# Scaling and saving the first two experts' weights on other engines and at other times, and routing the first batch right behind its convolution

## The chip, the cores and the metric

The kernel runs on one core of a Trainium2 chip. Each core has a matrix engine (TensorE, "PE"), a vector engine (VectorE, "DVE"), a scalar engine (ScalarE, "ACT"), a general engine (GpSimd, "POOL") and an engine that here only issues transfers (SyncE, "SP"). Every engine works through its own list of instructions in order, and waits at an instruction until what it needs is there. POOL also issues the transfers that gather and scatter rows. The metric is the device time of one execution in microseconds; lower is better.

## The reference: a causal convolution, then a mixture of experts

There are 8 sequences (batches) of 3584 tokens with 192 channels. Each of 8 heads convolves its 24 channels with 7 softmaxed taps. The result, 28672 rows, is then routed: a token with a positive skip score goes to the expert with its largest gate logit, and the expert's output, weighted by its gate probability, is added to the row.

```python
w = exp(weight - max); w = w / (sum(w) + 1e-9)          # 8 heads x 7 taps
out = einsum('hk,bskhg->bshg', w, x_unf)                # causal windows of 7 tokens
do_compute = x @ w_skip > 0
e_idx = argmax(xc @ w_gate); gate_w = softmax(...)[e_idx]
h = maximum(xc[mask] @ w1[e], 0)                        # 192 -> 1024
y[mask] = gate_w * (h @ w2[e])                          # 1024 -> 192
out[do_compute] = xc + y
```

## The kernel before, in words

**Two phases.** Phase one goes through the 8 batches (`phase1_step(b)`, b from 0 to 7). For each of the 8 heads of a batch, `conv_head` makes four fp32 matmuls into `pc` (line 301) and ACT copies them back over the input tile (line 304), so that the tile `xy` then holds the convolved rows. Phase two, "the tail", takes 64 blocks of up to 256 routed rows of one expert: POOL gathers their rows from DRAM (line 713), DVE and ACT split them into two fp16 parts (`prep`), SP transposes these by DMA (line 748), PE multiplies by W1 in `up` (line 792), ACT and DVE split the hidden values into `hh` and `hl` (lines 796 and 798), PE multiplies by W2 in `down` (lines 826 to 828), and POOL scatters the sums (line 810).

**Routing of a batch** is a chain written as generators that hand control back at each yield. `router` transposes the convolved rows on PE (line 356), copies them on ACT (line 357), multiplies by the gate weights (lines 363 and 366) and transposes the logits back (line 374). POOL makes an intermediate copy `yc` (line 337). `slots` works out on DVE which expert a token has (`lm` at line 412 to the one-hot `oh` at line 432), counts them with three matmuls (`pr`, lines 437 to 439), and gives each token its slot. Its line 445 also starts the store of the batch to DRAM (`store_y`, line 318). `invert` then turns slots into lists of rows: DVE builds one-hot tiles `oa`, `oj` and `ob` (lines 521 and 530) four times per batch, and PE sums them into `inv` (line 508). After batch 4 (`REL`), `tail_rows` reads `inv` and makes the row lists `rowsa` for the first 8 blocks, which belong to experts 0 and 1 (`NTAIL` is 8); they take the tokens of the batches up to 4. The next blocks of the two take rows from all batches.

**Weights.** The weights of an expert arrive as fp32 (`raw`, line 208) and are used as two fp16 parts. `split_weights(e, wt)` takes the maxima of seven pieces of 512 columns on DVE (line 216), a maximum over the partitions on POOL (`partition_all_reduce`, line 224), then makes a power of two scale `ar`, and for each of the seven pieces a scaled fp16 "high part" (for experts 0 and 1 on POOL, line 238; for the others on ACT, line 241) and the rest as the "low part" on DVE (`low_part`, line 254). There is one `raw` buffer. `save_weights` copies the finished parts of experts 0 and 1 to DRAM (`wscr`, line 262); the last blocks of the tail read any expert's weights from there.

**The order** is written out by tables of digits, one string per batch and one digit per head: `RR` says how often the routes are advanced behind that head, `IR` how often the inversion, `BGS` how many steps of the background list `bg` are run, which holds the generators of the weights. Before, a batch's route begins in the step of the following batch, one hop per head, so that PE's list alternates between the convolution of batch b, the transposes of batch b-1 and the inversion of batch b-2 or b-1. The order of each engine's instructions follows from the order in which these generators emit. `E1` is the batch in which the weights of expert 1 begin. In the tail, `background()` runs one step per slot.

**Buffers that tie the phases.** There are four row buffers for the batches, so batch b+4 is loaded when batch b is stored. The gather buffers `y` lie where the rows of batches 0 and 4 were; POOL clears them first (line 691). The buffers `hh` and `hl` lie where batches 1 and 5 were, so that the first `hh` of the tail waits until the last piece of batch 5 has landed in DRAM. A transfer that SP issues also waits until the transfer eight before it has landed.

Of the kernel before, what the change touches and what calls it, by code (L numbers as in the profile page):

```python
# [41 lines left out]
NA = 2  # L42
# [16 lines left out]
FIRST = ("0", "", "1", "", "2", "3", "", "")  # L59
WARM = (6, 58)  # L60

IR = ("00000000",) * 2 + ("11111112",) * 4 + ("11122222", "11111111")
RR = ("00000000",) + ("11111111",) * 7
BGS = ("40000000", "00000000", "11111111", "11122222", "11140000", "11111111", "11222222", "11111111")
PICK = "102"
E1 = 4
PIECES = (2,) * 5 + (8,) * 3

PSEQ = (0, 0, 3, 4, 4, 4, 4, 4)
# [20 lines left out]
def conv_router_moe(ctx: ExitStack, tc: tile.TileContext, x, band, taps, router_weights, weights, out):  # L90
    nc = tc.nc
# [57 lines left out]
    wra, wrb = wr[:, 0:2], wr[:, 2]  # L149
    nc.sync.dma_start(out=wr.rearrange("p j e -> p (j e)"), in_=router_weights)  # L150
    load_x(1)
    load_x(2)
    nc.vector.tensor_reduce(out=wkm, in_=wk, axis=AX.X, op=ALU.max)

    def over(t, n):
# [47 lines left out]
    def split_weights(e, wt):  # L203
# [30 lines left out]
        for k, (c0, c1, oh, ol, n) in enumerate(parts):  # L234
            for v in range(n):
                o = 512 * v
                if e < NA:
                    nc.gpsimd.tensor_scalar(out=wt[:, oh + o:oh + o + 512], in0=raw[:, c0 + o:c0 + o + 512],  # L238
                                            scalar1=ar[:, k:k + 1], scalar2=None, op0=ALU.mult)
                else:  # L240
                    nc.scalar.activation(wt[:, oh + o:oh + o + 512], raw[:, c0 + o:c0 + o + 512], AF.Copy,
                                         scale=ar[:, k:k + 1])
                if held:
                    low_part(*held)
                held = wt, raw, ar, e, k, c0 + o, oh + o, ol + o
                yield
                if e >= NA and (k, v) < (1, 1):
                    yield
# [336 lines left out]
    wts = {}  # L585
    bg = []
# [38 lines left out]

    def phase1_step(b):

        if b > 0:
            routes.append(whole_route(b - 1))
        if b in (0, E1):  # L630
            e = int(b == E1)
            wts[e] = new_wt(e)
            bg.append(split_weights(e, wts[e]))
        for h in range(H):
            if b > 0:
                conv_head(b, h)
            elif h == 0:
                first_batch()
            for i in range(max(int(RR[b][h]), int(IR[b][h]))):
                more = i < int(IR[b][h])  # L640
                if i < int(RR[b][h]):
# [14 lines left out]
            store_piece()  # L656
            if h == 6 and 2 <= b < B - 2:
                load_x(b + 2)
        if not b:
            load_x(3)  # L660

    def step7(h):

# [385 lines left out]
    ahead = []  # L1049
    while preps or begun[0] < PREP0:  # L1050
        prep_piece()
    bg.extend(save_weights(e, wts[e]) for e in range(NA))
    weave(up(blocks[0], weights_of(0)))
    for n in range(NBLK):
        k = blocks[n]
        if n == NTAIL:
            while not past:
                next(tables[0])
# [130 lines left out]
```

## Time and profile before

| | |
|---|---|
| median of 3 runs | 687.71 us (686.76 to 687.85) |
| profiled execution | 686.38 us, its span 684.7 us |
| mean granted TensorE clock | 0.967 |
| busy in the span: PE, DVE, ACT, POOL | 634.8, 490.5, 333.5, 290.1 us |
| phase one, to the first W1 matmul of the tail | 0 to 183.81 us |
| transition, PE all but idle | 187 to 193.71 us |
| tail | 193.71 to 684.7 us |
| moved by DMA | 136.87 MB, mean 200 GB/s |

In the rows of a timeline the first number is the start in microseconds from the span's start, the second the duration of the group, then come the engine, the line, the operation, the tile written and the tiles read, and xN the count; in brackets stands how long the engine had been idle before, and what ended that. In a table of stretches, each engine has its busy time and in brackets its instructions, PEclk is the granted clock as a share of full speed, DMA the mean busy share of the DMA engines. "issue" as a releaser means that the engine waited for nothing that the profile shows. A displayed duration holds some start-up that overlaps with the instruction before, so the distance between the starts of neighbours is a little shorter than the duration.

### The profile page before, as it was taken

The page shows a single profiled execution, that of the slowest core. Times are in us where ns is not written, and L with a number is a line of the kernel's source. Part 1 is how long each engine was busy: PE and PEld are TensorE (multiplying, and loading weights), DVE is VectorE, ACT ScalarE, POOL GpSimd, SP SyncE. Part 2 cuts the span into 40 slices and gives each one's busy share as a digit, 9 for nine tenths or more (in the row PEclk, how much of TensorE's full clock was granted, in tenths as well). Part 3 has the DMA queues.
Part 4 walks back from the last instruction along what each step waited for, and adds up shares of the span by engine and source line. Part 5 has one row for each costly group of instructions (what it writes and reads, how often), then busy time and mean ns, then how long its engine had stood idle before and what let it go on. Part 6 is the DMA issues. An engine that isn't in the chain of part 4 may idle for free.

```text
span 684.7 us, 18082 instructions
## 1 busy us (share of the span) xinstructions
PE 634.8 (93%) x6921; PEld 528.1 (77%) x6921; DVE 490.5 (72%) x1365; ACT 333.5 (49%) x666; POOL 290.1 (42%) x306
## 2 busy tenths in 40 slices
PE   7799599948769999999999999999999999999995
PEld 4456355524358999989999899999999899999995
DVE  2069397847758989787798788789788876666652
ACT  4587447734454333464463554554553634444321
POOL 2011441137204446365454554654555455554322
PEclk9999869998889999999999999999999999999998
DMA  8968659832586626276457365366464445999960
GB/s 354 424 269 351 256 195 412 316 129 73 143 325 214 205 65 193 63 202 188 79 171 194 82 183 179 109 166 162 126 207 118 119 140 174 297 313 292 288 206 15
DMA packets 93392, 136.87 MB, mean 200 GB/s; under 512 B 58300, under 2 KB 72574, under 8 KB 90864
## 3 DMA queue, kind: packets, MB, share of 16 engines
q1 hardware_dynamic: 82256, 112.92, 50.9%
q0 software_dynamic: 11040, 22.71, 11.8%
q8 instruction: 56, 0.92, 0.6%
q14 instruction: 40, 0.33, 0.2%
HBM read 73.24 MB, written 51.88 MB: 183 GB/s over the span
## 4 chain that ended last, share of the span: by engine, by line
PE 65%; DVE 5%; DMA 2%; POOL 1%; issue 1%; ACT 1%; SPq 1%; POOLq 0%; DVEq 0%; ACTq 0%
PE ph L792 29%; PE po L828 10%; PE po L826 10%; PE po L827 10%; PE ph L783 4%; DMA y<-out_dram,rowsa 1%; DVE hl L798 1%; PE tp L356 1%; POOL wt L238 1%; DVE oa L521 1%; DMA out_dram<-xy 0%; DVE yam L732 0%; ACT hh L796 0%; DVE yt L745 0%; POOL y L691 0%
## 5 line engine op out<-in xcount | busy, mean ns | idle before, releaser
L796 ACT ACTIVATE hh<-ph 128x512 f16<-128x512 f32 x230 | 130.8, 589 | 240.7 <-PE ph L792 227.7
L798 DVE SCALAR_TENSOR_TENSOR hl<-ph,hh 128x512 f16<-128x512 f32 x230 | 155.7, 685 | 57.1 <-ACT hh L796 55.4
L826 PE MATMUL po<-wt,hh 128*128 128x192 f16 x768 | 188.9, 246 | 0.0
L828 PE MATMUL po<-wt,hl 128*128 128x192 f16 x768 | 188.9, 246 | 0.0
L827 PE MATMUL po<-wt,hh 128*128 128x192 f16 x768 | 188.9, 246 | 0.0
L792 PE MATMUL ph<-m,wt 128*128 128x256 f16 (+1 forms) x1680 | 186.6, 269 | 1.0 <-DVE hl L798 0.6
L792 PEld LDWEIGHTS <-wt 128*128 128x128 f16 x1680 | 154.1, 98 | 26.3 <-issue 10.1
L810 POOL DMA_INDIRECT out_dram<-o,rows x82 | 87.3, 1065 | 126.4 <-DVE o L808 103.2
L713 POOL DMA_INDIRECT y<-out_dram,rows x82 | 85.2, 1039 | 25.5 <-issue 11.9
L827 PEld LDWEIGHTS <-hh 128*128 128x128 f16 x920 | 90.0, 98 | 0.6
L826 PEld LDWEIGHTS <-hh 128*128 128x128 f16 x920 | 90.0, 98 | 0.6
L828 PEld LDWEIGHTS <-hl 128*128 128x128 f16 x920 | 90.0, 98 | 0.0
L808 DVE SCALAR_TENSOR_TENSOR o<-po,yf,y 128x192 f32<-128x192 f32 x115 | 47.1, 415 | 48.7 <-PE po L828 46.3
L304 ACT COPY xy<-pc 128x768 f32<-128x768 f32 (+1 forms) x72 | 51.7, 728 | 44.1 <-PE pc L301 33.7
L301 PE MATMUL pc<-xy,toep 64*64 64x384 f32 (+1 forms) x576 | 61.0, 505 | 7.3 <-DMA xy<-in_x_dram 5.8
L745 DVE SCALAR_TENSOR_TENSOR yt<-y,ysc,yt 128x64 f16<-128x64 f32 x230 | 57.9, 311 | 2.9 <-ACT yt L740 2.9
L740 ACT ACTIVATE yt<-y,ysc 128x192 f16<-128x192 f32 x115 | 46.3, 447 | 22.6 <-DVE ysc L735 14.0
L254 DVE SCALAR_TENSOR_TENSOR wt<-raw,ar,wt 128x512 f16<-128x512 f32 x56 | 44.6, 806 | 13.6 <-POOL wt L238 13.6
L356 PEld LDWEIGHTS tp<-ident,xy 128*128 128x128 f32 x256 | 30.3, 151 | 25.2 <-issue 10.8
L337 POOL COPY yc<-xy 128x1024 f32<-128x1024 f32 x12 | 13.3, 1107 | 82.5 <-ACT xy L304 43.8
L356 PE MATMUL tp<-ident,xy 128*128 128x128 f32 x256 | 38.4, 297 | 6.6 <-ACT ya L357 6.6
L216 DVE TENSOR_REDUCE am<-raw 128x1 f32<-128x512 f32 x56 | 37.8, 676 | 2.0 <-DMA raw<-in_weights_dram 1.6
(183 smaller groups left out, 827.9 us busy)
## 6 DMA issues: line engine op xcount, KB each, us to landing
xy<-in_x_dram SPq DMA_DIRECT2D x7, 3200.0 KB
wd<-wscr SPq DMA_DIRECT2D x44, 449.0 KB
wscr<-wt SPq DMA_DIRECT2D x84, 128.0 KB
out_dram<-xy SPq DMA_DIRECT2D x21, 400.0 KB
raw<-in_weights_dram SPq DMA_DIRECT2D x16, 512.0 KB
out_dram<-xy SPq DMA_DIRECT2D x5, 1600.0 KB
out_dram<-xy SPq DMA_DIRECT2D x5, 1500.0 KB
raw<-in_weights_dram SPq DMA_DIRECT2D x16, 384.0 KB
```

The lines of the kernel that those rows point to most:

```text
L301: nc.tensor.matmul(pc[K1 * c:K1 * c + K1, r, 0:n * G], toep[K1 * r:K1 * r + K1, h, :], xy[K1 * r:K1 * r + K1, at:at + 2 * n - 1:2, h * G:( ...
L304: nc.scalar.copy(xy[:, 2 * i0:2 * i0 + 2 * n, h * G:(h + 1) * G].rearrange("p (i r) g -> p r i g", r=2), pc[:, :, 0:n * G].rearrange("p r ...
L356: nc.tensor.transpose(tp[:, u, :], src, ident)
L713: rows_apart(nc.gpsimd.indirect_dma_start(out=k.y[:, u, :], out_offset=None, in_=out[0:k.rows, :], in_offset=bass.IndirectOffsetOnAxis(ap= ...
L745: nc.vector.scalar_tensor_tensor(out=yt[:, u, o:o + b_ - a], in0=k.y[:, u, a:b_], scalar=sc[:, u:u + 1], in1=yt[:, u, a:b_], op0=ALU.mult, ...
L792: nc.tensor.matmul(ph[:, f - f0, :], wt[:, o + f * P:o + (f + 1) * P], k.m[:, m, 0:w], start=(n == 0 and not paired(k)), stop=(n == len(se ...
L796: nc.scalar.activation(hh, ph, AF.Relu)
L798: nc.vector.scalar_tensor_tensor(out=k.hl[:, f0:f0 + fs, 0:w], in0=ph, scalar=0.0, in1=hh, op0=ALU.max, op1=ALU.subtract)
L810: rows_apart(nc.gpsimd.indirect_dma_start(out=out[0:k.rows, :], out_offset=bass.IndirectOffsetOnAxis(ap=k.si[:, u:u + 1], axis=0), in_=o[: ...
L826: nc.tensor.matmul(pos[u], hh, w2(OW2, f), start=(f == 0), stop=False)
L827: nc.tensor.matmul(pos[u], hh, w2(OW2L, f), start=False, stop=False)
L828: nc.tensor.matmul(pos[u], hl, w2(OW2, f), start=False, stop=(f == NF - 1))
```

## The change

Four things are done at once.

- The loads of batches 2 and 3 are issued behind the load of expert 0's weights; before, batch 2 was ahead of these weights.
- The whole router of batch 0 is emitted in step 0, behind its convolution and ahead of the convolution of batch 1; its slots and its inversion begin in step 1. From batch 1 on, a route begins one step later, as before.
- The high parts of experts 0 and 1 are scaled on DVE instead of POOL. Their steps lie elsewhere: expert 0's maxima in steps 1 and 2 (before: step 2) and its scaling in step 3 (before: the end of step 3 and step 4), expert 1 begins in step 3 (before 4) and is scaled in step 6, one piece per head (before: in the last heads of step 6).
- The two experts' parts are saved to DRAM from the sixth block of the tail on (`n == NTAIL - 3`) instead of at its head.

```diff
-IR = ("00000000",) * 2 + ("11111112",) * 4 + ("11122222", "11111111")
-RR = ("00000000",) + ("11111111",) * 7
-BGS = ("40000000", "00000000", "11111111", "11122222", "11140000", "11111111", "11222222", "11111111")
+IR = ("00000000",) + ("11111112",) * 5 + ("11122222", "11111111")
+RR = ("11111111",) * 8
+BGS = ("00000000", "00111111", "11111111", "22222400", "11111111", "11111111", "11111111", "11111111")
 PICK = "102"
-E1 = 4
+E1 = 3
...
     load_x(1)
-    load_x(2)
...
                 if e < NA:
-                    nc.gpsimd.tensor_scalar(out=wt[:, oh + o:oh + o + 512], in0=raw[:, c0 + o:c0 + o + 512],
+                    nc.vector.tensor_scalar(out=wt[:, oh + o:oh + o + 512], in0=raw[:, c0 + o:c0 + o + 512],
                                             scalar1=ar[:, k:k + 1], scalar2=None, op0=ALU.mult)
...
     def phase1_step(b):
 
-        if b > 0:
+        if b > 1:
             routes.append(whole_route(b - 1))
         if b in (0, E1):
             e = int(b == E1)
             wts[e] = new_wt(e)
             bg.append(split_weights(e, wts[e]))
+        if b == 0:
+            background(4)
+            load_x(2)
+            load_x(3)
+            first_batch()
+            routes.append(whole_route(0))
         for h in range(H):
             if b > 0:
                 conv_head(b, h)
-            elif h == 0:
-                first_batch()
...
-        if not b:
-            load_x(3)
...
-    bg.extend(save_weights(e, wts[e]) for e in range(NA))
     weave(up(blocks[0], weights_of(0)))
     for n in range(NBLK):
         k = blocks[n]
+        if n == NTAIL - 3:
+            bg.extend(save_weights(e, wts[e]) for e in range(NA))
```

The change moves instructions on every engine. Three places follow, as the lists of the two kernels have them; line numbers of the changed kernel are one lower than before around here.

**PE, where the convolution of batch 0 ends** (`xy_102` is batch 0, `xy_180` batch 1). Before:

```order
L301 MATMUL pc_7_8_322<-xy_102,toep 64x192 x4
L301 MATMUL pc_0_0_335<-xy_180,toep 64x384 x4
L356 MATMUL tp_0_0_343<-ident,xy_102 128x128 x4
L356 MATMUL tp_0_1_349<-ident,xy_102 128x128 x4
L301 MATMUL pc_1_0_355<-xy_180,toep 64x384 x4
```

Of the change, the end of batch 0's router, after which the convolution of batch 1 begins:

```order
L355 MATMUL tp_1_5_430<-ident,yc_1_376 128x128 x4
L362 MATMUL pl_1_436<-ya_1_378,wr 32x256 x8
L365 MATMUL pl_1_436<-yb_1_423,wr 32x256 x4
L373 MATMUL pb_1_451<-ident,lt_1_449 128x128 x2
L300 MATMUL pc_0_0_456<-xy_180,toep 64x384 x4
L300 MATMUL pc_1_0_476<-xy_180,toep 64x384 x4
L436 LDWEIGHTS ones_105
L436 MATMUL pr_482<-oh_474,ones_105 128x31x8
L437 MATMUL pr_482<-hist,ones_214 128x8
```

The twelve groups of transposes and the products of batch 0 now stand in front of the first matmul that reads batch 1, and the convolution of batch 1 is interrupted by batch 0's counts (`pr`) and, further on, its inversion.

**DVE, where the low parts of expert 0's weights are made** (`raw_328` and `raw_230` are its fp32 weights, `raw_982` expert 1's; `oa`, `oj` and `ob` are the one-hot tiles of an inversion, the last of which PE waits for). Before, where step 3 passes into step 4, with the scaling itself on POOL:

```order
L530 TENSOR_TENSOR ob_8_990<-oj_8_989,vals_918 128x576
L254 SCALAR_TENSOR_TENSOR wt_231<-raw_328,ar_768,wt_231 128x512 x2
L521 TENSOR_TENSOR oa_16_1044<-ramp,rf_914 128x1024
L521 TENSOR_TENSOR oj_16_1045<-iota_j,qf_916 128x576
L530 TENSOR_TENSOR ob_16_1046<-oj_16_1045,vals_918 128x576
```

Of the change, in step 3, ahead of the first and second `ob` of batch 1:

```order
L520 TENSOR_TENSOR oa_0_936<-ramp,rf_929 128x1024
L520 TENSOR_TENSOR oj_0_937<-iota_j,qf_931 128x576
L237 TENSOR_SCALAR wt_229<-raw_230,ar_651 128x512
L253 SCALAR_TENSOR_TENSOR wt_229<-raw_230,ar_651,wt_229 128x512
L237 TENSOR_SCALAR wt_229<-raw_230,ar_651 128x512
L253 SCALAR_TENSOR_TENSOR wt_229<-raw_230,ar_651,wt_229 128x512
L529 TENSOR_TENSOR ob_0_938<-oj_0_937,vals_933 128x576
L237 TENSOR_SCALAR wt_229<-raw_230,ar_651 128x512
L253 SCALAR_TENSOR_TENSOR wt_229<-raw_230,ar_651,wt_229 128x512 x2
L520 TENSOR_TENSOR oa_8_1008<-ramp,rf_929 128x1024
L520 TENSOR_TENSOR oj_8_1009<-iota_j,qf_931 128x576
L211 MEMSET am_1020 128x8
```

Scalings (L237) and low parts (L253) alternate on DVE, and behind the last low part and the next `oa` and `oj` follows the first maximum of expert 1's weights, ahead of the second `ob`. In step 6 the same seven pairs of expert 1 stand one per head between the pieces of batch 3's and batch 4's inversions.

**SP, where the tail begins** (`xy_1031` and `xy_1049` are batch 5, `xy_1325` and `xy_1333` batch 6). Before:

```order
L748 DMA_TRANSPOSE m_2275<-yt_2272 128x3x128 x2
L318 DMA out_dram<-xy_1031 128x800 x2
L262 DMA wscr<-wt_231 128x1024 x2
L318 DMA out_dram<-xy_1031 128x600
L262 DMA wscr<-wt_231 128x1024 x5
L262 DMA wscr<-wt_231 128x16
L318 DMA out_dram<-xy_1325 128x800
```

Of the change:

```order
L749 DMA_TRANSPOSE m_2275<-yt_2272 128x3x128 x2
L317 DMA out_dram<-xy_1049 128x800 x2
L317 DMA out_dram<-xy_1049 128x600
L317 DMA out_dram<-xy_1333 128x800 x4
L749 DMA_TRANSPOSE m_2625<-yt_2593 128x3x128
```

The last piece of batch 5 (128x600) now follows the other pieces directly, with no save between. The saves come further on in SP's list, directly ahead of the load of expert 2's weights.

## The prediction

> **What bounds the kernel now.** I read first the busy time by stretch, one row per batch of phase one (each from a batch's first convolution matmul to the next batch's), then the transition and the start of the tail.
>
> ```profile
> core 0: us, PE busy (x) PEld busy (x) DVE busy (x) ACT busy (x) POOL busy (x), PEclk, DMA share, GB/s
> 21.56:39.21 17.65, 17.65 (x165) 9.58 (x165) 0.00 (x0) 12.97 (x24) 1.04 (x1) 0.90 0.98 414
> 39.21:56.95 17.74, 17.69 (x185) 9.98 (x184) 16.35 (x44) 14.04 (x28) 2.08 (x2) 1.00 0.56 218
> 56.95:74.98 18.03, 18.03 (x202) 10.77 (x199) 11.86 (x40) 13.79 (x28) 2.68 (x3) 1.00 0.86 350
> 74.98:107.48 32.50, 23.13 (x202) 13.27 (x199) 22.29 (x50) 14.08 (x28) 14.71 (x9) 0.74 0.66 254
> 107.48:125.51 18.03, 18.03 (x202) 10.77 (x199) 16.18 (x45) 13.79 (x28) 2.08 (x2) 1.00 0.81 343
> 125.51:154.50 28.99, 19.19 (x218) 11.55 (x215) 18.94 (x51) 14.34 (x30) 8.99 (x7) 0.95 0.57 222
> 154.50:183.81 29.31, 22.43 (x182) 11.41 (x181) 22.41 (x68) 16.48 (x34) 15.89 (x21) 0.82 0.31 83
> 183.81:193.71 9.90, 3.35 (x32) 2.85 (x31) 3.55 (x11) 1.32 (x5) 0.20 (x3) 0.94 0.94 338
> 193.71:300.00 106.29, 104.87 (x1197) 95.38 (x1198) 91.19 (x300) 48.04 (x98) 48.70 (x54) 0.97 0.55 169
> ```
>
> An undisturbed batch takes 18.03 us and fills PE. Batch 4 (32.50) and batch 6 (28.99) are longer, batch 7 is long too, and the transition leaves PE idle. From 193.71 on PE is nearly full (104.87 of 106.29), so a microsecond won before that point should be won in the end. Next the timelines of PE, POOL and DVE in batches 4 and 6.
>
> ```profile
> 84.89 0.40 PE L508 MATMUL inv<-ob,oa 128*128 128x72 f16 x4 [8.01 <-DVE ob L530]
> 142.71 0.42 PE L508 MATMUL inv<-ob,oa 128*128 128x72 f16 x8 [2.60 <-DVE ob L530]
> 153.99 0.58 PE L508 MATMUL inv<-ob,oa 128*128 128x72 f16 x7 [7.06 <-DVE ob L530]
> ...
> 80.36 1.19 DVE L254 SCALAR_TENSOR_TENSOR wt<-raw,ar,wt 128x512 f16<-128x512 f32 x1 [6.84 <-POOL wt L238]
> ...
> 78.75 9.97 POOL L238 TENSOR_SCALAR wt<-raw,ar 128x512 f16<-128x512 f32 x6 [7.17 <-ACT ya L357]
> 140.43 0.37 POOL L224 PARTITION_ALL_REDUCE sc<-ar  x1 [7.05 <-issue]
> ```
>
> PE waits for the one-hot tile `ob`; DVE, in order, holds `ob` back behind a low part (L254) that waits for POOL's scaling. POOL sits idle for 7 us ahead of each of the two operations and then takes 9.97 / 6 = 1.66 us per piece. The scaling on POOL is thus what ends last in both batches.
>
> **The change part by part.** I walk through the batches; T1 is the start of batch 1's convolution, and so on.
>
> Router of batch 0 alone. It starts where the last convolution matmul of batch 0 ends, 16.81 + 0.94 = 17.75.
>
> ```profile
> 16.81 0.94 PE L301 MATMUL pc<-xy,toep 64*64 64x192 f32 x16 [0.21 <-ACT xy L304]
> 21.56 1.31 PE L301 MATMUL pc<-xy,toep 64*64 64x384 f32 x8 [3.81 <-DMA xy<-in_x_dram]
> 22.79 1.97 PE L356 MATMUL tp<-ident,xy 128*128 128x128 f32 x8
> 25.76 1.09 PE L356 MATMUL tp<-ident,xy 128*128 128x128 f32 x8
> 31.25 1.09 PE L363 MATMUL pl<-ya,wr 128*32 128x256 f32 x16
> ...
> 30.25 1.08 ACT L357 COPY ya<-tp 128x512 f32<-128x512 f32 x2
> ```
>
> Twelve groups of transposes cost PE 0.55 each and ACT 0.54; with two PSUM buffers I take 0.67 (between 0.55, overlapped, and 1.1, in series): 8.0. The two products (1.09 plus the 0.36 of their second part) and the copies that must end before the next matmul add 3.9. T1 = 17.75 + 11.9 = 29.65; batch 1 had landed by 21.56, and nothing is put ahead of it. (Batch 2 now loads behind expert 0's 1.8 MB: some 12 MB at 414 GB/s, landed near 31, are needed at 43.) Then DVE's chain for batch 0 runs beside nothing but eight convolutions. Its length is read from batch 3's chain.
>
> ```profile
> 57.54 0.41 DVE L412 TENSOR_REDUCE lm<-lg 128x31 f32<-128x248 f32 x1 [0.68 <-ACT lg L376]
> ...
> 66.37 0.68 DVE L521 TENSOR_TENSOR oa<-ramp,rf 128x1024 f16<-128x1024 f16 x1
> 67.45 0.46 DVE L530 TENSOR_TENSOR ob<-oj,vals 128x576 f16<-128x576 f16 x1
> ...
> 70.83 0.29 PE L508 MATMUL inv<-ob,oa 128*128 128x72 f16 x4
> 137.64 0.42 PE L508 MATMUL inv<-ob,oa 128*128 128x72 f16 x8
> ```
>
> From `lm` to the end of the first `ob` are 67.91 - 57.54 = 10.4, which holds 1.1 of an older inversion; in batch 1 two maxima (1.3) stand there instead. So `ob` is ready at about 40.6, PE (needing 8.3 for the whole batch) waits some 5, and the second `ob` ends 2.5 later: T2 = 43.4. Batch 2 then takes a full batch without counts, 17.0 (the 17.65 of the first row without its slow start), so T3 = 60.4 against 56.95: **+3.4**. Bounds: -3.4 (PE never waits) to +9.4 (transposes in series, DVE chain unshared).
>
> Scaling on DVE. No row shows it; the nearest are a copy of 1024 fp32 and the two kinds of 512.
>
> ```profile
> L339 DVE COPY yc<-xy 128x1024 f32<-128x1024 f32 x1 | 0.7, 686 | 0.0
> ...
> 93.04 0.74 DVE L254 SCALAR_TENSOR_TENSOR wt<-raw,ar,wt 128x512 f16<-128x512 f32 x1
> 93.69 0.66 DVE L449 TENSOR_TENSOR_SCAN run<-smask,pr 128x248 f32<-128x248 f32 x1
> ...
> 96.14 0.34 SPq L208 DMA_DIRECT2D raw<-in_weights_dram x1
> 100.82 0.69 DVE L216 TENSOR_REDUCE am<-raw 128x1 f32<-128x512 f32 x1 [1.38 <-DMA raw<-in_weights_dram]
> ```
>
> Half the copy is 0.33; a piece with two tensor inputs takes 0.65 from start to start. One input from SBUF is the copy's case, so I take 0.33; a pair costs 0.98. The Trainium skill, "VectorE: DVE Perf Modes", "Mode 2×_2P", gives fp32 tensor_scalar two results per cycle, which by that page's overhead makes an estimate of about 0.42 and would put the sum some 1 us later; no run here shows it yet.
>
> Batch 3 now holds six scalings and five low parts ahead of its first `ob`: 0.6 (start of `lm`) + 10.4 - 1.1 + 0.35 + 1.98 + 3.25 = T3 + 15.4. PE could use it at 13.9 - 0.9 = 13.0 (70.83 less the older inversion): a wait of 2.4. Behind it one more scaling, two low parts, `oa`, `oj`, and then the first maximum of expert 1's weights, whose load may only be issued after the last low part, at T3 + 17.0. Before, issue to maximum took 100.82 - 96.14 = 4.7 beside a store; I take 4.0. Everything behind that maximum waits in DVE's list, the second `ob` first: T4 = T3 + 22.4, **+4.4** (bounds +3 to +7). Batches 4 and 5 are undisturbed at 18.03: **-14.5** in batch 4. Batch 5 already had 16.18 us of DVE work in 18.03 without a wait.
>
> Batch 6: three pairs ahead of its first `ob`: 0.6 + 10.4 + 2.9 + 0.2 = 14.1 against PE's 137.64 - 125.51 = 12.1. The other three follow at 2.4 each (a pair and 1.4), so T7 = T6 + 21.7: **-7.3** (bounds -4 to -10.9, the undisturbed 18.03).
>
> Batch 7. POOL is free before the batch ends, so its clears lie in batch 6, and the row list `rowsa` no longer stands behind low parts.
>
> ```profile
> 163.22 0.18 DVE L578 SCALAR_TENSOR_TENSOR rowsa<-cmp,dec 128x16 int32<-128x16 f32 x1
> 170.74 0.56 DVE L732 TENSOR_REDUCE yam<-y 128x2 f32<-128x386 f32 x1 [3.52 <-DMA y<-out_dram,rowsa]
> ...
> 186.43 1.05 SPq L318 DMA_DIRECT2D out_dram<-xy x2
> 187.52 1.53 SPq L262 DMA_DIRECT2D wscr<-wt x2
> 189.10 0.65 SPq L318 DMA_DIRECT2D out_dram<-xy x1
> 192.59 0.60 ACT L796 ACTIVATE hh<-ph 128x512 f16<-128x512 f32 x1 [8.58 <-DMA out_dram<-xy]
> ```
>
> `rowsa` ends 8.9 after the batch's start; by its chain alone 0.6 + 2.7 + 1.1 + 0.6 = 5.0. What is late next, gather, `yam`, ACT's `yt` and the transposes, keeps its distances: **-3.9** (bounds -1.5 to -6). Transition: without the two saves (1.53) the last store piece is issued 1.57 earlier and has 0.5 MB less beside it: **-2.0** (bounds 0 to -3; nothing if another transfer lands last).
>
> The saves in the tail, 16 transfers of 3.7 MB, now lie in SP's list ahead of four later transposes and of expert 2's load.
>
> ```profile
> 255.02 3.92 SPq L208 DMA_DIRECT2D raw<-in_weights_dram x4
> 262.87 0.69 DVE L216 TENSOR_REDUCE am<-raw 128x1 f32<-128x512 f32 x1
> ```
>
> The load has 7.9 us before its first use, and the queues move 169 GB/s there against 414 in batch 1, so 3.7 MB need some 10 us of which about 8 go by while they are issued: **0**; without that cover, DVE stands up to 3 us at that maximum, with `hl` behind it. Removed POOL switches (7 us each) matter only where counted.
>
> PE's clock falls after waits: the eight transposes at 22.79 took 1.97 after 3.81 idle, 1.09 later. The new waits (5 in two pieces in batch 1, about 2 each in batches 3 and 6) may cost one such start: **+1.5** (0 to +6.4, four of 1.6).
>
> Sum: 3.4 + 4.4 - 14.5 - 7.3 - 3.9 - 2.0 + 1.5 = **-18.4**. On the profiled 686.38 (1.70 above its span of 684.7) that is 668.0; the median of the runs is 1.33 higher, so **669.3**.
>
> **The rivals.**
>
> *Half clock and dear DVE starts* (18%). Each of four new waits is followed by a slow start, 6.4 instead of 1.5, and expert 1's load takes the full 4.7: 675 to 681. For it: the clock of 0.74 in batch 4. Against: after the 2.60 at 142.71 eight matmuls took 0.42, as the eight at 137.64. The Trainium skill, "TensorE: Matmul & The Clock Gate", "Part 1: The HAM clock gate", says the clock halves after an idle window of about 3.4 us; the row after 3.81 us agrees, and whether the shorter waits do it no run shows. By that rule only batch 1's wait counts, as in my sum.
>
> *DVE keeps up* (18%). Transposes and inversions lie so that batches 3 and 6 run at 18.03 with the load landing early: 4.4 + 3.7 less, and no slow start: 659 to 664. Against: the counted DVE work of batch 6, 18.94 and seven scalings.
>
> *DVE becomes the bound* (8%), the case on the other side. If a scaling costs on DVE what it costs on POOL, 1.66, each of the seven in batches 3 and 6 lies on the path with 1.33 more, together 18.6, which brings 688, no change; if the low parts also keep the 1.19 of the row at 80.36 instead of 0.65, 7.6 more, 695. It is slower from about 1.75 per scaling. Against: the low part at 93.04, free of POOL, is back at 0.74, and a scaling reads less than it does.
>
> *The scaling does not leave the path* (1%): batch 4 waits for expert 0 as before; 687.
>
> **How the numbers follow.** Forecast 55% with its own range 664 to 675, the rivals as said. 660 to 680 leaves out the lower part of the second rival (6%), the top of the first (4%) and the last two (9%). A measurement tells 0.2% (1.4 us) from no change. The third rival is half no change, half slower; with the fourth: faster 0.91, same 0.05, slower 0.04.
>
> **What would show it.** Right: PE idle 5 to 9 us between 17.75 and 45, the first tail matmul near 167, no wait of PE above 3.5 us between batches 3 and 6, scalings under 0.45, `rowsa` 5 us into batch 7, one POOL idle of 6 to 7 us in place of five. Wrong: batch 1 waiting for its input, a batch 3 above 25, scalings above 0.7, a first `hh` that waits for a store as long as before, DVE idle at expert 2's first maximum, or a tail longer than the present 492.1 us (684.7 - 192.59) from its first `hh`.

## The result and the profile after

The changed kernel takes **677.37 us** (median of 4 runs, 675.37 to 679.07) against 687.78 for the kernel before on the same chip: ratio **0.9845, 95% interval 0.981 to 0.9881**. The profiled execution took 676.47 with a span of 674.8. The forecast was 669.3 with 660 to 680. The sign is right and the range holds the time, but the gain is 10.4 us and not 18.4, and the time lies outside the 664 to 675 that the forecast gave its own mechanism. An execution that took longer at a lower granted clock than the others of its kernel (one of e10, one of the kernel before on chip C) is left out of all medians and ratios.

The stretches of the changed kernel, cut as the prediction cut those of before (batches 1, 2, 3, 4, 6, 7, the transition, and 20 us of the tail):

```profile
core 0: us, PE busy (x) PEld busy (x) DVE busy (x) ACT busy (x) POOL busy (x), PEclk, DMA share, GB/s
29.07:44.18 15.11, 9.79 (x85) 3.59 (x84) 13.86 (x41) 6.39 (x11) 0.00 (x0) 0.82 0.98 403
44.18:61.42 17.24, 17.24 (x182) 9.66 (x180) 3.31 (x7) 13.13 (x25) 2.08 (x2) 0.96 0.67 267
61.42:85.34 23.92, 19.59 (x185) 10.56 (x184) 19.49 (x54) 14.70 (x30) 3.08 (x4) 0.93 0.48 180
85.34:104.00 18.66, 18.36 (x203) 10.76 (x200) 17.55 (x48) 13.40 (x25) 1.54 (x2) 1.00 0.93 385
...
122.03:145.48 23.45, 20.38 (x217) 12.42 (x215) 22.08 (x56) 13.95 (x28) 2.08 (x2) 0.93 0.77 292
145.48:169.93 24.45, 20.53 (x184) 10.53 (x182) 16.59 (x63) 16.79 (x37) 11.14 (x17) 0.86 0.37 113
169.93:178.20 8.27, 3.35 (x33) 2.86 (x32) 3.50 (x11) 1.32 (x5) 0.20 (x3) 0.82 0.62 214
...
240.00:260.00 20.00, 15.85 (x200) 14.49 (x198) 13.44 (x51) 4.39 (x9) 11.78 (x14) 0.93 0.97 276
```

PE resumes after the transition at 178.20 instead of 193.71, so phase one gained 15.5. But the span is only 9.9 shorter: the rest of the program takes 496.6 (674.8 - 178.20) instead of 491.0 (684.7 - 193.71). **5.6 us are lost in the tail**, and the last row shows where: there PE works for 15.85 of 20 us, at a granted clock of 0.93, with the DMA engines busy for 0.97 of the time.

The timelines of the changed kernel behind those rows:

```profile
32.21 0.37 PE L436 MATMUL pr<-oh,ones 128*128 128x248 f16 x1 [1.63 <-DVE oh L431]
39.93 0.40 PE L507 MATMUL inv<-ob,oa 128*128 128x72 f16 x4 [3.42 <-DVE ob L529]
40.26 1.56 PE L300 MATMUL pc<-xy,toep 64*64 64x384 f32 x8
...
62.37 0.37 POOL L223 PARTITION_ALL_REDUCE sc<-ar  x1 [10.52 <-ACT lg L375]
62.77 0.98 DVE L272 TENSOR_SCALAR sc<-sc 128x2 f32<-128x2 f32 x1 [15.28 <-POOL sc L223]
67.25 0.48 DVE L237 TENSOR_SCALAR wt<-raw,ar 128x512 f16<-128x512 f32 x1
67.64 0.48 DVE L237 TENSOR_SCALAR wt<-raw,ar 128x512 f16<-128x512 f32 x1
78.50 0.29 PE L507 MATMUL inv<-ob,oa 128*128 128x72 f16 x4 [2.37 <-DVE ob L529]
79.53 1.85 PE L362 MATMUL pl<-ya,wr 128*32 128x256 f32 x16
81.09 1.14 PE L365 MATMUL pl<-yb,wr 128*32 128x256 f32 x8
83.89 0.69 DVE L215 TENSOR_REDUCE am<-raw 128x1 f32<-128x512 f32 x1 [2.73 <-DMA raw<-in_weights_dram]
85.00 0.42 PE L507 MATMUL inv<-ob,oa 128*128 128x72 f16 x8 [0.96 <-DVE ob L529]
...
112.03 0.35 POOL L223 PARTITION_ALL_REDUCE sc<-ar  x1
128.86 1.54 DVE L253 SCALAR_TENSOR_TENSOR wt<-raw,ar,wt 128x512 f16<-128x512 f32 x1
137.17 0.42 PE L507 MATMUL inv<-ob,oa 128*128 128x72 f16 x8 [3.07 <-DVE ob L529]
137.52 1.40 PE L300 MATMUL pc<-xy,toep 64*64 64x384 f32 x8
...
177.07 0.60 ACT L797 ACTIVATE hh<-ph 128x512 f16<-128x512 f32 x1 [6.95 <-DMA out_dram<-xy]
...
217.59 3.96 SPq L749 DMA_TRANSPOSE m<-yt  x2
...
239.99 7.27 SPq L261 DMA_DIRECT2D wscr<-wt  x10
246.60 1.01 DVE L746 SCALAR_TENSOR_TENSOR yt<-y,ysc,yt 128x64 f16<-128x64 f32 x4
247.31 1.47 SPq L207 DMA_DIRECT2D raw<-in_weights_dram  x2
248.94 2.50 SPq L749 DMA_TRANSPOSE m<-yt  x2
256.98 0.28 PE L784 MATMUL ph<-m,wt 64*128 64x256 f16 x1 [4.00 <-DMA m<-yt]
```

In phase one the picture is the predicted one: PE waits for one-hot tiles in batches 1, 3 and 6, DVE waits once for expert 1's weights, and of POOL's long idle times ahead of a reduction or a scaling only one is left, 10.52 at 62.37. In the tail, SP issues the last ten saves, half of expert 2's load and then two transposes. Their source `yt` is ready at 247.61 (246.60 + 1.01), so SP issues them only 1.3 us late; but they land 8 us after the first of them is issued, and PE waits 4.00 us for their tile `m`.

### The profile page after: what moved, and what is told of

Same layout as the page of the kernel before. It is cut to its first block, busy times and chain, and to the rows that moved or that the text cites. A ratio compares the mean times of both kernels' runs of the same rounds, so it can differ in the third digit from the quotient of the medians.

```text
span 674.8 us, 18071 instructions
## 1 busy us (share of the span) xinstructions
PE 633.5 (94%) x6921; PEld 526.3 (78%) x6921; DVE 488.8 (72%) x1379; ACT 333.8 (49%) x666; POOL 265.3 (39%) x292
## 4 chain that ended last, share of the span: by engine, by line
PE 77%; DVE 11%; DMA 5%; ACT 3%; issue 2%; SPq 1%; POOL 0%; POOLq 0%; ACTq 0%; DVEq 0%
PE ph L793 29%; PE po L829 10%; PE po L827 10%; PE po L828 10%; PE pc L300 5%; PE tp L355 4%; PE ph L784 4%; PE pl L362 2%; DMA m<-yt 2%; DVE wt L253 1%; DVE hl L799 1%; DMA xy<-in_x_dram 1%; DVE oa L520 1%; PE inv L507 1%; ACT xy L303 1%
## 5 line engine op out<-in xcount | busy, mean ns | idle before, releaser
L300 PE MATMUL pc<-xy,toep 64*64 64x384 f32 (+1 forms) x576 | 59.6, 499 | 3.8 <-DMA xy<-in_x_dram 2.0
L355 PEld LDWEIGHTS tp<-ident,xy 128*128 128x128 f32 x256 | 28.2, 143 | 21.2 <-ACT ya L356 9.3
L253 DVE SCALAR_TENSOR_TENSOR wt<-raw,ar,wt 128x512 f16<-128x512 f32 x56 | 42.0, 759 | 0.0
L355 PE MATMUL tp<-ident,xy 128*128 128x128 f32 x256 | 35.8, 284 | 5.4 <-ACT ya L356 5.2
```

What stands on the lines that cost most here:

```text
L300: nc.tensor.matmul(pc[K1 * c:K1 * c + K1, r, 0:n * G], toep[K1 * r:K1 * r + K1, h, :], xy[K1 * r:K1 * r + K1, at:at + 2 * n - 1:2, h * G:( ...
L355: nc.tensor.transpose(tp[:, u, :], src, ident)
```

## The experiments

All runs in one table. Runs of one letter share a chip and their runs of the kernel before (A 704.2, B 686.0, C 687.34, D 686.4; chip A is slower for every kernel; B and C have the same chip number). "First hh" is the start of ACT's first `hh`, "tail" the profiled span less that start; these two compare across B, C, D and the runs of the result (before: 192.59 and 492.1; changed: 177.07 and 497.7).

| run | chip | what | median us | ratio to before (95%) | first hh | tail |
|---|---|---|---|---|---|---|
| e1 | A | changed, saves at the head of the tail | 687.03 | 0.9761 (0.9707-0.9816) | 175.67 | 505.5 |
| e2 | A | changed, saves in batches 6 and 7 | 684.20 | 0.9729 (0.9665-0.9794) | 177.46 | 504.8 |
| e3 | A | changed, saves issued by ACT | 690.18 | 0.9791 (0.9745-0.9838) | 175.53 | 510.1 |
| e4 | A | before, scaling on DVE | 682.67 | 0.9688 (0.9615-0.9761) | 175.26 | 506.7 |
| e5 | B | changed, again | 677.46 | 0.9872 (0.984-0.9904) | 177.19 | 497.9 |
| e6 | B | changed, late router | 674.48 | 0.9836 (0.9802-0.987) | 174.51 | 498.1 |
| e7 | B | changed, reduction primed at the start | 677.76 | 0.9882 (0.9846-0.9919) | 177.22 | 497.0 |
| e8 | B | e4, batch 5 stored in two pieces | 662.91 | 0.9651 (0.962-0.9681) | 171.30 | 490.4 |
| e9 | C | e8, reduction primed later | 658.03 | 0.9592 (0.9557-0.9627) | 163.75 | 490.7 |
| e10 | C | e9, expert steps spread | 655.26 | 0.9524 (0.9486-0.9563) | 164.88 | 490.6 |
| e11 | C | e8, the two stores issued by ACT | 661.76 | 0.9625 (0.9595-0.9655) | 171.23 | 490.3 |
| e12 | D | changed, saves from the third block | 677.57 | 0.9864 (0.9836-0.9892) | 177.75 | 498.9 |

### Where the tail's 5.6 us come from: the saves (e1, e2, e3, e12)

**e1**, the saves back at the head of the tail:

```diff
+    bg.extend(save_weights(e, wts[e]) for e in range(NA))
     weave(up(blocks[0], weights_of(0)))
...
-        if n == NTAIL - 3:
-            bg.extend(save_weights(e, wts[e]) for e in range(NA))
```

> The changed kernel with the saves back at the head of the tail (one part undone). Its own trace has 8.27 us of transition (169.93 to 178.20) and 496.6 us from there to the end; before these were 9.90 and 491.0. Theory A, the saves stand in SP's list ahead of expert 2's load and of transposes, whose tile m then lands late (PE waits 4.00 us for it at 256.98 and has a lower clock behind it): the tail goes back to about 491, the transition to about 9.9, together 672 to 673. Rival B, the tail is longer for another reason, such as its earlier start: the tail stays at 496, the transition still grows, 678.

**e2**, one save step per head in the first four heads of batch 6 (expert 0) and of batch 7 (expert 1), none in the tail:

```diff
             background(int(BGS[b][h]))
+            if b in SAVE1 and h < 4:
+                if not h:
+                    saving.append(save_weights(SAVE1.index(b), wts[SAVE1.index(b)]))
+                next(saving[-1], None)
```

> The changed kernel with the saves of expert 0 issued in the first four heads of batch 6 and those of expert 1 in the first four of batch 7, where the DMA engines are busy 0.77 and 0.37 of the time. Theory A (the place in SP's list among the transposes is what cost 5.6 us): transition as in the changed kernel, 8.3, tail about 491, batches 6 and 7 unchanged, 671. Rival B (the tail is longer for another reason): 676 to 677. Rival C (the saves delay batch 7's stores and gathers by the 9 us that 3.7 MB take at 400 GB/s, half of it hidden): 675 to 676 with a batch 7 or a transition longer by 4.

**e3**, the same place as in the change, another issuer:

```diff
-            nc.sync.dma_start(out=wscr[e, :, c:min(c + 1024, WW)], in_=wt[:, c:min(c + 1024, WW)])
+            nc.scalar.dma_start(out=wscr[e, :, c:min(c + 1024, WW)], in_=wt[:, c:min(c + 1024, WW)])
```

> The changed kernel with the same saves at the same place in the program, issued by ACT instead of SP. Theory A in the form 'SP issues transposes only behind 16 saves and they land behind these in one queue': the wait of 4.0 us for m falls under 1, the tail is 491 to 492, 671. Rival B, bandwidth: 3.7 MB and expert 2's 1.8 MB share the 16 DMA engines with the transposes whichever engine issues them: PE still waits 3 to 4 us for m, 676.

Chip A is slower in the tail for all of them, so the absolute times that were expected did not come; what compares are the tails on this chip. With the saves at the head the tail is 505.5, in phase one 504.8, in the kernel before with DVE scaling (saves at the head too) 506.7, and with the saves in block six, issued by ACT, 510.1. The last is 3.4 to 5.3 longer, but it has another issuer as well, and no run on chip A has SP issue the saves in block six. What speaks for the place is the wait itself: PE's longest wait for a transposed tile in the tail is 1.3 us in e1 and 1.7 in e2, against 4.00 in the changed kernel. That the queue is to blame (A of e3) is not borne out: with ACT issuing them PE still stands just ahead of the same product.

```profile
258.58 0.28 PE L784 MATMUL ph<-m,wt 64*128 64x256 f16 x1 [2.55 <-issue]
```

The profile names no releaser there, so that PE waited for `m` is likely but not shown; shorter idle times of this kind, up to 1.1 us, stand in e1 and e4 too.

The Trainium skill, "DMA: Bandwidth & Descriptors", "Issuing engines are not separate DMA queues", says that transfers of all issuers run on the same 16 DMA engines; e3 does not speak against it, but there ACT's own `hh` also stands behind the DMAs that ACT issues (ACT is idle for 4.74 ahead of the one at 247.88), so which of the two cost the time is open. e2 did not gain in the transition either: its first `hh` is at 177.46.

**e12**, the changed kernel with the saves three blocks earlier:

```diff
-        if n == NTAIL - 3:
+        if n == NTAIL - 6:
```

> The changed kernel with the saves from the third block of the tail on instead of the sixth, so that SP has issued them all some three transposes before expert 2's load. Theory A (it is 3.7 MB of saves directly ahead of 1.8 MB of load, with the next transposes behind both, that makes the tile m late): PE no longer waits 3.6 to 4.2 us for m near 257, the first hh stays at 177, the tail from it is 491 to 493 instead of 497.7, 4 to 6 us less than the changed kernel: a ratio to before of 0.976 to 0.980 (the changed kernel had 0.9845 and 0.9872 on two chips). Rival: the collision only moves, transposes between 203 and 230 wait behind the saves and the stores of batch 7 instead, or expert 2's load alone makes m late: a wait of PE of 3 us or more for m stays, 0.983 to 0.988.

The rival came: the tail is 498.9, the wait for `m` near 257 is gone, and one of 4.21 us stands at 230 instead.

```profile
218.05 1.00 DVE L746 SCALAR_TENSOR_TENSOR yt<-y,ysc,yt 128x64 f16<-128x64 f32 x4
221.76 1.72 SPq L261 DMA_DIRECT2D wscr<-wt  x2
223.52 0.95 SPq L317 DMA_DIRECT2D out_dram<-xy  x1
224.63 3.34 SPq L749 DMA_TRANSPOSE m<-yt  x2
...
222.37 1.25 PE L793 MATMUL ph<-m,wt 128*128 128x256 f16 x10 [0.67 <-DVE hl L799]
230.07 2.29 PE L793 MATMUL ph<-m,wt 128*128 128x256 f16 x10 [4.21 <-DMA m<-yt]
```

So the collision with expert 2's load is not what decides. The pair of transposes at 224.63 is the one that the changed kernel issued from 217.59 on: six saves and the store pieces between them now hold SP up ahead of it, its data land 5.4 us later, and PE, ready at 225.86 (230.07 - 4.21), waits. Here the source `yt` is ready at 219.05 and the pair is issued 5.6 us after that, where the pair behind the saves of the changed kernel was issued after 1.3 and took 8.0 to land. In the changed kernel it is thus the landing that is slow; in e12 the late issue takes part too, and how much of the wait is due to each these runs do not show. The ten matmuls behind the wait take 2.29 instead of 1.25, so the wait costs PE more than itself. In all five profiles with SP's saves in block six or three (the changed kernel, e5, e6, e7, e12) PE waits 3.6 to 4.2 us for `m`. In e8 to e11, where they stand at the head, PE waits for no DMA in the tail and the tail is 490.3 to 490.7: only one transpose stands among the saves there, and nothing waits for its tile.

### Which part of the change brings the gain (e4, e5, e6)

**e4**, the kernel before with one word changed (`nc.gpsimd.tensor_scalar` to `nc.vector.tensor_scalar` at L238).

> The kernel before with one part of the change alone: the scaling on DVE. All else as before (order of loads, router of batch 0, steps, saves). By the terms of my sum batch 4 loses 13 to 14 us, batch 6 about 7, batch 7 about 4, nothing is paid for the early router, for batch 3 or in the tail: 662 to 665, faster than the changed kernel by 12 to 15. Rival: the moved steps of the change are needed for the gain (the pairs lie at the end of step 3 and in step 4 ahead of the one-hot tiles, expert 1's in the last heads of step 6), batch 4 stays above 24 and batch 7 above 28: 672 to 680.

It takes 21.5 us less than before on its chip (23 to 26 were expected), 0.9688 of it: faster than the whole change (0.9845, and 0.9872 in e5), with intervals that do not meet. But e4 and those two were timed on different chips; the nearest pair on one chip is e8, which is e4 with one thing more, and e5 (below). Its batch 4 takes 24.53, as the rival asked (above 24); its batch 7 stays below the rival's 28, at 27.36. Its batch 7 begins at 138.42 (before 154.50; changed kernel 145.48, e5 145.59 and e12 146.27 on other chips). Two things keep it from the time expected, in batch 4 and at the end of phase one:

```profile
79.36 0.29 PE L508 MATMUL inv<-ob,oa 128*128 128x72 f16 x4 [1.31 <-DVE ob L530]
83.84 0.37 PE L437 MATMUL pr<-oh,ones 128*128 128x248 f16 x1 [2.36 <-DVE oh L432]
175.26 0.60 ACT L796 ACTIVATE hh<-ph 128x512 f16<-128x512 f32 x1 [9.28 <-DMA out_dram<-xy]
176.38 1.97 PE L356 MATMUL tp<-ident,xy 128*128 128x128 f32 x8 [7.25 <-ACT ya L357]
```

ACT waits 9.28 us for a store of batch 5: of the 7.1 us by which batch 7 began earlier than in the changed kernel, only 1.8 are left at the first `hh`.

**e5** is the changed kernel again, as a measure on chip B.

> The changed kernel again, unchanged, beside three others on the chip of this call (the chips differ: on that of the first call the kernel before took 704.2 us, 687.8 in the run of the result). Expected if the changed kernel behaves as in its own trace: PE's restart near 178.2, a wait of about 4 us for m near 257, and a ratio to before of 0.976 to 0.988. If that wait was an accident of one run, the trace here has none and the tail is 4 to 5 us shorter than that of the changed kernel with ACT issuing the saves (508.9).

It repeats the trace: the restart at 178.31, a wait of 3.7 for `m`, a tail of 497.9. The wait is no accident.

**e6**, the router of batch 0 back in step 1:

```diff
-IR = ("00000000",) + ("11111112",) * 5 + ("11122222", "11111111")
-RR = ("11111111",) * 8
+IR = ("00000000",) * 2 + ("11111112",) * 4 + ("11122222", "11111111")
+RR = ("00000000",) + ("11111111",) * 7
...
-        if b > 1:
+        if b > 0:
...
-            routes.append(whole_route(0))
```

> The changed kernel with the router of batch 0 back in step 1 and its slots and inversion from step 2 on (the loads stay in the new order). Theory: the early router costs what the traces put on it, T3 = 61.42 against 56.95; here T1 returns to about 21.6 to 22 and T3 to 57 to 58, the scaling steps lie where they did, so the first expert maximum and all of batch 3 keep their 23.9, and the end comes 4 earlier than the changed kernel's: 0.994 of it. Rival: expert 0's 1.8 MB ahead of batch 2 now keep PE waiting for its input, T3 at 60 or later, no gain.

674.48 against 677.46, with intervals that overlap a little, and the profile agrees: batch 3 starts at 57.81 instead of 61.90 in e5, the first `hh` is at 174.51 instead of 177.19. The rows are the first convolution of batch 3, in e5 and in e6:

```profile
61.90 0.88 PE L300 MATMUL pc<-xy,toep 64*64 64x384 f32 x8
```

```profile
57.81 0.88 PE L300 MATMUL pc<-xy,toep 64*64 64x384 f32 x8
```

So 4.1 us of the early router arrive at batch 3 and 2.7 at the first `hh`, and the new order of the loads makes no batch wait. What then still parts e6 from e4 in phase one, the moved steps of the experts and the order of the loads, costs 4.4 us at batch 7 (142.79 against 138.42) and nothing at the first `hh` (174.51 against 175.26).

### POOL's late reduction (e7, e9)

**e7**, a reduction of a dummy tile among the constants:

```diff
     nc.gpsimd.memset(ones32, 1.0)
+    prime = const.tile([P, 2], F32, name="prime")
+    nc.gpsimd.memset(prime, 1.0)
+    nc.gpsimd.partition_all_reduce(prime, prime, P, bass.bass_isa.ReduceOp.max)
```

> The changed kernel with one more operation, a reduction over partitions on POOL of a dummy tile among the constants at the start. Theory: the 10.5 us that POOL stands idle ahead of the reduction at 62.37 are the first use of that operation, so they are paid at the start beside the first loads; sc is ready by 53, DVE has no 15.28 us of idle time, ob of batch 3 is 1.5 earlier, PE's wait for it falls from 2.37 to about 0.9 and has no lower clock behind it, batch 3 takes 20 to 22 instead of 23.9: 2 to 4 us less than the changed kernel. Rival: the copies in between evict it, POOL idles 6 to 10 us again ahead of the reduction, no difference.

```profile
21.66 0.37 POOL L202 PARTITION_ALL_REDUCE prime<-prime  x1 [10.38 <-issue]
23.37 1.09 PE L358 MATMUL tp<-ident,yc 128*128 128x128 f32 x8 [3.27 <-POOL yc L339]
55.27 0.35 POOL L226 PARTITION_ALL_REDUCE sc<-ar  x1
```

The long idle time belongs to the first use: it stands ahead of the dummy, and the real reduction follows a copy without one. But the early router needs POOL's copy `yc` right then, so batch 1 starts 4.3 later (33.53 against 29.21 in e5). Batch 3 becomes 1.3 shorter, not 2 to 4, since PE still waits 2.35 for `ob`. Nothing is won: 677.76.

**e9** puts the dummy where POOL has room, in e8's kernel (below):

```diff
             background(int(BGS[b][h]))
+            if (b, h) == (1, 3):
+                prime = const.tile([P, 2], F32, name="prime")
+                nc.vector.memset(prime, 1.0)
+                nc.gpsimd.partition_all_reduce(prime, prime, P, bass.bass_isa.ReduceOp.max)
```

> The kernel of the run before (scaling on DVE, batch 5 stored in two pieces, the rest as before; 662.9 us, ratio 0.9651) with a reduction over partitions of a dummy tile on POOL behind batch 0's two copies, at about 31 us, where POOL then has 10 us without work. Theory: the reduction of expert 0 no longer waits 5.92 us, DVE does not stand still 3.6 us at sc in batch 3, and PE's waits of 1.09 and 2.36 us in batch 4, with the lower clock behind them, go: batch 4 takes 18 to 20 instead of 23.8, 4 to 5 us less, 658 to 659 (0.958). Rival 1: what PE waits for in batch 4 is the number of scalings ahead of lm, not their start: no change, 663. Rival 2: the load of the operation is slow there beside the input loads and the copies of batch 1 come late: slower, as in the changed kernel with the reduction among the constants (yc waited for it, T1 4.3 later).

```profile
38.94 0.37 POOL L654 PARTITION_ALL_REDUCE prime<-prime  x1 [8.99 <-ACT lt L369]
90.83 0.29 PE L508 MATMUL inv<-ob,oa 128*128 128x72 f16 x4 [1.46 <-DVE ob L530]
```

Here it pays. Batch 4 takes 19.99 instead of 23.79, one wait of 1.46 is the longest left in it, and 658.03 came as forecast. In the traces the first `hh` is 7.6 earlier than in e8; 1.5 of that stand ahead of the dummy already (batch 2 begins at 39.20 instead of 40.67) and are not its work.

### What ended the transition (e8, e11, e10)

**e8** is e4 with `PIECES = (2,) * 6 + (8,) * 2`: batch 5 is stored in two pieces.

> The kernel before with the scaling on DVE (it restarted PE at 176.38) and batch 5 stored in two pieces instead of eight, so that its last piece is issued in the second head of batch 7, ahead of the transposes and of the saves. Theory: the transition is set by the last piece of batch 5, whose place in SP's list behind six transposes and two saves makes it land at 175; with it gone the first hh is free as soon as its product ends, near 167, and PE restarts at 169 to 171: 5 to 7 us less than with the scaling alone, 0.959 to 0.962 of before. Rival: the next block's transposed rows or POOL's clears of o come no earlier, PE waits for them instead, and the end moves by less than 2.

```profile
160.18 0.44 PE L374 MATMUL pb<-ident,lt 128*128 128x128 f32 x2 [4.22 <-ACT lt L369]
171.30 0.60 ACT L796 ACTIVATE hh<-ph 128x512 f16<-128x512 f32 x1 [1.15 <-issue]
```

662.91 against 677.46 for the changed kernel on the same chip. `hh` no longer waits for a store and comes 4.0 earlier than in e4. More was forecast: PE now waits 4.22 at 160.18 for ACT, which stands behind gathered rows that come later (SP's first transposes are at 161.97, in e4 at 158.18).

**e11** lets ACT issue these two pieces, two heads later (`nc.scalar` for `b == B - 3` in `store_y`, no piece in the first two heads of batch 7).

> The kernel with the scaling on DVE and batch 5 in two pieces, with these two pieces issued by ACT in the third and fourth head of batch 7 instead of by SP in front of the transposes. In the kernel with SP they start at 146.93, one microsecond ahead of the gathers, and the gathered y lands at 157.3 (PE then waits 4.22 us at 160.18); in the one with scaling alone the first transposes were issued 3.8 us earlier (158.18 against 161.97). Theory: the gathers go ahead of 3.2 MB, y lands 3 to 4 us earlier, PE's wait of 4.22 goes: 3 us less than 662.9 (0.961). Rival: the stores then land later than the first hh needs them (171.3), the transition's wait is back: 663 to 666.

```profile
159.27 0.69 PE L374 MATMUL pb<-ident,lt 128*128 128x128 f32 x2 [2.73 <-ACT lt L369]
```

PE's wait falls from 4.22 to 2.73 but `hh` stays at 171.23, and 0.9625 against 0.9651 is within the intervals. A late gather is thus not all that sets this point.

**e10** is e9 with `BGS` of steps 3 to 6 as `"11122211", "11132000", "11112222", "11111111"`.

> The same with the steps of the experts spread: two of expert 0's scalings go from the end of step 3 into step 4, and expert 1's preparation is four steps earlier in step 5, so that its scalings lie one per head in step 6 instead of two per head. Theory: PE's wait of 2.64 us for oh in batch 7 and the 0.70 in batch 6 come from pairs standing ahead of lm on DVE; they go, with the lower clock after 144.35: 3 to 4 us less than the kernel with the late reduction alone, 655 to 656. Rival: DVE's work only lies elsewhere, batch 5 or 6 waits for it by as much, or the rows' chain of batch 7 is set by the gathers (157.3 for y) and gives it back: within 1 us.

PE's waits of 2.6 and 0.7 around the start of batch 7 are gone as expected, yet the first `hh` is no earlier (164.88 against 163.75):

```profile
92.94 0.40 PE L508 MATMUL inv<-ob,oa 128*128 128x72 f16 x4 [2.27 <-DVE ob L530]
153.40 0.69 PE L374 MATMUL pb<-ident,lt 128*128 128x128 f32 x2 [5.04 <-ACT lt L369]
```

Batch 4 waits instead, and batch 7 waits 5.04 where e9 waited 2.25. The median of 655.26 is what was forecast, but the trace is that of the rival: the waits only lie elsewhere. The two medians differ by 2.8 with intervals that overlap a little; whether the spread helps is not settled. Both are some 20 us faster than the changed kernel.

## Why the prediction was right and where it failed

The step that failed is "**The saves in the tail ... 0**". It asked only whether expert 2's load would be late, found 7.9 us of cover for it, and priced a miss as DVE waiting at the maximum. DVE waited 1.2 us for that load in all, 1.02 of it at the first maximum. The transposes, which the same passage names as standing behind the saves, were given no price. They carry the tile that PE needs next, and both places tried in the middle of the tail show the cost: 497.0 to 498.9 from the first `hh`, against 490.3 to 492.1 with the saves at the head (chip A apart). Two of the prediction's signs of being wrong came: a tail longer than 492.1 (497.7), and DVE idle at expert 2's first maximum. The cover itself was too small: of 414 GB/s the 169 already moved leave 245, at which 3.7 MB need 15 us and not some 10. The Trainium skill, "DMA: Bandwidth & Descriptors", "Queues, rings and completion order", says that each DMA engine takes the descriptors of one issuer in order; the transposes that land 8 us after issue behind saves and load agree with it, and by that rule the question should have been what stands behind the saves.

The terms of phase one, measured from the starts of the batches:

| term | forecast | measured | what differed |
|---|---|---|---|
| router alone and batch 1, to T3 | +3.4 | +4.5 | T1 29.07 (29.65), waits 1.63 and 3.42 as said; lower clock behind |
| batch 3 | +4.4 | +5.9 | `sc` late |
| batch 4 | -14.5 | -13.8 | 18.66; 18.03 in e5 |
| batch 6 | -7.3 | -5.5 | one low part at 1.54, lower clock |
| batch 7 | -3.9 | -4.9 | |
| transition | -2.0 | -1.6 | |
| slow starts, apart | +1.5 | in the rows above | |
| tail | 0 | +5.6 | |

Phase one missed by 2.9 (15.5 gained of 18.4), the tail by 5.6. The mechanism of phase one was right: scaling on DVE takes 0.48, and 0.39 from start to start (67.25 and 67.64), against the 0.33 taken and the 0.42 estimated from the Trainium skill's "VectorE: DVE Perf Modes", "Mode 2×_2P"; expert 1's load came 3.7 after its issue against 4.0; PE's long waits of 8.01 in batch 4 and 7.06 in batch 6 are gone as said. Three signs of being right were missed by a little: the first matmul of the tail is at 169.93 and not near 167, a scaling shows 0.48 and not under 0.45, and POOL's idle time is longer (below).

PE's wait in batch 3, 2.37 against 2.4, was right by luck: the first `ob` came 1.6 later than forecast, but PE was ready 1.7 later too (76.13, T3 + 14.7 instead of 13.0).

**The clock term** foresaw one slow start of 1.5, and three came: three groups of eight convolutions at 1.56 instead of 0.88 in batch 1 and at the start of batch 2 (2.0), 1.85, 1.14 and 1.16 instead of 1.09, 0.64 and 0.88 in batch 3 (1.5), and 1.40, 0.69 and 1.91 instead of 0.88, 0.44 and 1.09 in batch 6 (1.6), 5.1 in all. But most of this was not on the path. The same list of phase one ran in e1 and e5, and there some of the waits are not followed by a lower clock. Batch 6 of e1, then batch 3 of e5:

```profile
119.80:142.69 22.89, 19.08 (x217) 11.40 (x214) 21.79 (x56) 14.35 (x30) 2.08 (x2) 1.00 0.86 329
134.95 0.42 PE L507 MATMUL inv<-ob,oa 128*128 128x72 f16 x8 [3.07 <-DVE ob L529]
...
61.90:86.08 24.18, 18.02 (x185) 9.98 (x184) 19.48 (x54) 14.71 (x30) 3.44 (x4) 1.00 0.50 185
78.88 0.29 PE L507 MATMUL inv<-ob,oa 128*128 128x72 f16 x4 [2.35 <-DVE ob L529]
85.73 0.42 PE L507 MATMUL inv<-ob,oa 128*128 128x72 f16 x8 [2.89 <-DVE ob L529]
```

Batch 6 took 22.89 at a clock of 1.00 and 23.45 at 0.93, so the slow start there cost 0.56. Batch 3 took 24.18 at 1.00 and 23.92 at 0.93: it cost nothing, since PE waits again for the second `ob`, 2.89 at full clock and 0.96 behind the slow matmuls. Batches 1 and 2 took 32.35 here and 31.39 in e1, with less time at the lower clock: 1.0 at least, 2.0 at most. Together that is 1.6 to 2.6 against the 1.5 of the sum. So the time of 677.37 lies among the 675 to 681 of the rival "half clock and dear DVE starts", but not for its reasons: its four starts at 1.6 on the path did not come, nor did a load of 4.7, and 5.6 of the missing gain lie in the tail, which it took as the forecast did. The rule of an idle window of about 3.4 us (the Trainium skill, "TensorE: Matmul & The Clock Gate", "Part 1: The HAM clock gate") does not hold here as a bound: waits of 2.37 and 3.07 were followed by a lower clock, while the same waits in e5 and e1 and one of 2.60 in the kernel before were not.

In batch 6 the first `ob` ended at 137.12, T6 + 15.1 instead of 14.1. One low part ahead of it, at 128.86, took 1.54 instead of 0.75, in e1 and e5 too; why is not shown.

Mis-sized was POOL's idle time ahead of its reduction, taken as 6 to 7 and measured as 10.52. With it `sc` came at 62.77, and the first `ob` of batch 3 ended at 78.45, T3 + 17.0 instead of 15.4. e7 shows that this is the first use of the operation and that removing it shortens batch 3 by 1.3 (against e5), most of the 1.5 by which batch 3 missed.

The rival "DVE becomes the bound" is refuted by the 0.48 per scaling; "the scaling does not leave the path" by batch 4, and by e4, in which this one line alone brings more than the whole change did on its chips. "DVE keeps up" failed at the waits of 2.37 and 3.07.

The sum also took for granted that what phase one has gained at batch 7 arrives at its end. Here it did (9.0 at batch 7, 15.5 with that batch's own gain and the transition's), but the place where it ends is a store of batch 5 behind transposes in SP's list, and kernels that reach batch 7 earlier give part of it back there (e4 is 7.1 ahead at batch 7 and 1.8 at `hh`).

## What to carry to other kernels

When transfers are moved in a queue, list what stands behind them, and price each by the engine that needs it soonest; saves belong where no transfer behind them is awaited, and a cover worked out for one of these transfers says nothing about the next. Time each part of a combined change alone: here one changed word seems worth more than the whole (e4, and e8 against e5), since the early router and the moved saves cost some 3 and 5 us. And where a phase ends in a store in a queue, gains ahead of it shrink until that store is moved.

## What was not expected of the hardware

- A lower clock behind PE waits of only 2.37 and 3.07 us, and none behind the same two waits (2.35 and 3.07) in e5 and e1, or behind the 2.60 in the kernel before. The length of the wait alone does not decide it; what does these runs do not show.
- The first reduction over partitions on POOL stood behind 10.4 to 10.5 us without work in the changed kernel (e5 10.43, e7 10.38), 9.0 in e9, and 5.9 to 6.1 in e8 and e4; what makes the difference is not shown. The second had none after copies (112.03 above), while in the kernel before, with scalings on POOL in between, it had 7.05 again.
- One chip took 704.2 for the kernel before and some 14 us more in the tail for every kernel profiled there, with granted clocks no lower (0.978 to 0.984) than elsewhere. In these four traces PE stands idle in the tail for 3 to 8 us in all with "issue" as releaser, and not at all so in the changed kernel's; this may be a part of the 14, the rest is not shown.
